# Row maxima of a gated attention kernel in two half-width matmuls: one single maximum a step, split between two places of the step

## The chip, the cores and the metric

The kernel runs on one core of a Trainium2 chip. The metric is the device time of one launch in microseconds (us). Engines are called TensorE (PE in the profile, its weight loads PEld), VectorE (DVE), ScalarE (ACT), GpSimd (POOL) and SyncE (SP); SyncE computes nothing here and issues DMAs.

## What is computed

The input x has 2048 rows of 512. Two attention branches with 32 heads of 16 read it, and a gate mixes their outputs:

```python
g = sigmoid((x * gate_w).sum(-1))
a = branch_A(x)      # 8 keys a query, at distances 0, 2, .. 14
# branch B: 32 heads of queries, one head of keys and values
q = (x @ wq) per head;  k = x @ wk;  v = x @ wv
p = softmax((q @ k.T) * 16 ** -0.5)       # 2048 keys for each query and head
b = (p @ v, heads side by side) @ wo
out = g * a + (1 - g) * b
```

Branch B's softmax needs the maximum of each row of 2048 scores before the exponential. The kernel computes the scores twice for that: once with queries on the partitions, only to take the maxima, and once with keys on the partitions, for the exponential.

## The kernel before, in words

**Units and steps.** Branch B is cut into 32 units (`NU`): 4 blocks of 512 queries times 8 groups of 4 heads. A unit has 16 steps (`NJ`), one for each 128 keys; 512 steps (`NS`) in all. Before a unit's first step its row maxima must be known: they are subtracted through two extra rows of the queries' operand `qst` (`shift_a`, `shift_c`, `shift_b`), so that the score matmuls of the second computation give shifted scores.

**A step** of the main loop (line 737 on) does: scores of the first two heads (`exp_pair`, L316, into a bank pair `pe`), their exponential on ScalarE (L318), scores and exponential of the other two heads, and the weighted sum of the step before (`weighted`, L326, four column tiles into `po`). The two heads of a pair lie on two row groups of the array (partitions 0 to 63 and 64 to 127), so that their matmuls run side by side.

**Maxima** are made in the gaps. A full set of maxima is 32 units x 32 slots; a slot is 512 keys for 128 queries of two heads. `fill_pair` (L269) makes a whole slot: two matmuls of 512 keys, one a row group, into the two banks of `m2` (called pm in the profile), and one VectorE reduce of 128x1024 (L274). `fill_one` (L278) makes half a slot, a "single": one matmul of 512 keys of one head into the one bank `m1` (called ps) and one reduce of 128x512 (L285). 64 such halves make a unit (`NF // NU`). In the step the order is written out: scores, pair, scores, single, weighted sum (`order`, L752; the first step after an output phase has the two scores swapped).

**Planner.** The order is fixed when the program is built, by hand-made clocks for TensorE, ScalarE and VectorE (`clk`, `after`) with the costs of line 42; `free` says when a bank is thought free. `fill_ready` makes a maximum if its bank is thought free within a slack (0.15) of TensorE's clock. `more` maxima as singles are made while the count still to make is above what the pairs alone would give (L766, L767). If a unit's maxima are late, `pause` makes them in the `pe` banks with nothing else going on. `tasks` are small pieces with a due time (shift, `finish_c`), run at the end of a step by `run_tasks`; `hooks` are those of branch A (`a_max`, `a_exp`, `a_sum`).

**When a unit's 64th half is made**, `filled` (L258) issues two small reduces (L264) and a 32x32 transposition (L266) on VectorE at once. ScalarE and VectorE then form the shift `ml` (L291, L297), and `shift_b` (L301) issues 8 small DMAs of it into `qst`: all on SyncE while branch A still has work on GpSimd, later 4 on SyncE and 4 on GpSimd.

**Around the steps.** A front stage (to about 316 us) makes the projections, with maxima of the first units between them; four output phases (`out_phase`) of 4 row blocks each multiply with wo, with pairs and singles between. Branch A runs on GpSimd beside all of this. SyncE also loads each unit's queries (`stack`, L231, two DMAs) and stores outputs (L501).

Of the kernel before, what the change touches and what calls it, by code (L numbers as in the profile page):

```python
# [13 lines left out]
P = 128  # L14
# [4 lines left out]
NJ = S // P  # L19
# [18 lines left out]
NS = NU * NJ  # L38
NF = 2 * NU * 2 * 4 * 4


T_R, T_LAT, T_EXP, T_RED2, T_RED1, T_W, T_LUMP, T_Q = 0.23, 0.20, 0.92, 1.14, 0.61, 1.18, 2.53, 3.2


@with_exitstack
def gated_mix_kernel(ctx, tc, xt, wa, wk, wq, wo_a, wo_b, out):
# [190 lines left out]
    slots += [(v, pr, t, kc) for v in range(2, NU) for pr in range(2) for t in range(4) for kc in range(4)]  # L237
    half = []
    free = {"m2": 0.0, "m1": 0.0, "e0": 0.0, "e1": 0.0, "po": 0.0}
    tasks, shifted = [], set()  # L240

    def fillable():
        return bool(half) or bool(slots) and slots[0][0] < len(stacked) and stacked[slots[0][0]] <= clk["pe"]
# [7 lines left out]
    def max_mm(dst, v, pr, t, kc, odd):  # L251
        b = 64 * odd
        nc.tensor.matmul(dst, qst[v % NB][b:b + 62, pr, t * P:(t + 1) * P], kst[b:b + 62, kc * 512:(kc + 1) * 512], start=True, stop=True)  # L253

    def to_go():
        return 2 * len(slots) + len(half)

    def filled(v, n):  # L258
        left[v] -= n
        if not left[v]:  # L260
            ms = wp.tile([P, 2, 2, 8], F32, name="ms")
            m = mx.pop(v).rearrange("p b i t k -> p b (i t) k")
            for x in range(2):
                nc.vector.tensor_reduce(ms[:, :, x, :], m, AX.X, ALU.max)  # L264
            mt = wp.tile([P, 32], F32, name="mt")
            nc.vector.transpose(mt, ms.rearrange("p b x y -> p (b x y)"))  # L266
            tasks.append((after("dve", 0, 0.5) + 0.1, shift_a, (v, mt)))

    def fill_pair(dst, key):  # L269
        v, pr, t, kc = slots.pop(0)  # L270
        m = unit_tile(v)
        for odd in range(2):
            max_mm(dst[:, odd, :], v, pr, t, kc, odd)
        nc.vector.tensor_reduce(m[:, :, pr, t, kc], dst, AX.X, ALU.max)  # L274
        free[key] = after("dve", after("pe", 0, T_R) + T_LAT, T_RED2) + 0.08
        filled(v, 2)

    def fill_one(dst=m1, key="m1"):  # L278
        if not half:
            v, pr, t, kc = slots.pop(0)  # L280
            half.extend([(v, pr, t, kc, 0), (v, pr, t, kc, 1)])
        v, pr, t, kc, odd = half.pop(0)
        m = unit_tile(v)
        max_mm(dst, v, pr, t, kc, odd)
        nc.vector.tensor_reduce(m[:, odd, pr, t, kc:kc + 1], dst, AX.X, ALU.max)  # L285
        free[key] = after("dve", after("pe", 0, T_R) + T_LAT, T_RED1) + 0.08
        filled(v, 1)

# [7 lines left out]
    def shift_c(v, mt, th, ml):  # L296
        nc.vector.scalar_tensor_tensor(ml, mt, mk[:, 5:6], th.bitcast(F32), op0=ALU.mult, op1=ALU.add)  # L297
        after("dve", 0, 0.2)
        shift_b(v, ml)

# [193 lines left out]
    def out_store(j, n, k):  # L494
# [4 lines left out]
        if n == C:  # L499
            nc.gpsimd.tensor_add(two[:, 0], two[:, 0], two[:, 1])  # L500
            nc.sync.dma_start(out[0].rearrange("(p j) d -> p j d", j=NJ)[:, j, :], two[:, 0])  # L501
# [57 lines left out]
    def fill_ready(key, slack):  # L559
        if fillable() and free[key] <= clk["pe"] + slack:  # L560
            clk["pe"] = max(clk["pe"], free[key])
            if key == "m1":
                fill_one()
            elif half and (not slots or half[0][0] < slots[0][0] or slots[0][0] >= len(stacked)):
                fill_one(m2[:, 0, :], "m2")
# [3 lines left out]
    def pause(most):  # L569
        n = 0  # L570
        while n < most and slots and fillable():
            key = min(("e0", "e1", "m2"), key=lambda k: free[k])
            clk["pe"] = max(clk["pe"], free[key])
            if half:
                fill_one({"e0": eb[0], "e1": eb[1], "m2": m2}[key][:, 0, :], key)
# [21 lines left out]

    def run_tasks():
        for task in [t for t in tasks if t[0] <= clk["pe"]]:
            tasks.remove(task)  # L600
            task[1](*task[2])

    def front_fills(slack, post=None, first=None):
# [36 lines left out]

    hooks, pool, done = [], 0.0, set()
    QK, AV = 12500, 22500
# [12 lines left out]
    def run_pool():  # L655
        nonlocal pool
        now = clk["pe"] * 1e3
        while pieces and pool < now + 3000:
# [13 lines left out]
            elif kind == "qk1":  # L672
                a_scores(g, 1)
                pool += QK
                hooks.append((pool + 6000, a_max, g, "max"))
            elif kind == "sub":
                a_sub(g)
                pool += 800
                hooks.append((pool + 4000, a_exp, g, "exp"))
                hooks.append((pool + 6500, a_sum, g, "sum"))  # L680
            elif kind == "wo":
# [3 lines left out]
            else:  # L685
                a_values(g)
                pool += AV
        for h in sorted(hooks, key=lambda h: h[0]):
            if h[0] <= now:
                hooks.remove(h)  # L690
                h[1](h[2])
                done.add((h[3], h[2]))

# [43 lines left out]
    for s in range(NS + 1):  # L737
# [9 lines left out]
        v = min(x[0][0] for x in (half, slots, [(NU,)]) if x)  # L747
        need = left.get(v, NF // NU)
        steps = 16 * v - 6 - s
        short = need - 2.8 * max(0, steps) if v < NU else 0  # L750
        lead = (NF - to_go()) / 64 - s / 16
        order = (0, "m2", 1, "m1") if s > 1 else (1, "m2", 0, "m1") if s else ()  # L752
        if not pieces and clk["pe"] * 1e3 > pool + 2000 and outs < NJ:
            n = C if outs < NJ - 4 else C - 1
            if s >= (16 * NHG * (outs // 4 + 1) + 4 if n == C else 16 * (NU - 2) + 4) and (lead < 1.6 or outs == 0 and s >= 400):
                out_phase(list(range(outs, outs + 4)), n)
                outs += 4
                order = (1, "m2", 0, "m1")
        elif short > 0 and steps < 2:
            pause(short)  # L760

        for which in order:
            if which == "m2":
                fill_ready("m2", 0.15)
            elif which == "m1":
                ahead = 2 * (16 * (NU - 2) - 8 - s) + 11 * (NJ - 4 - outs)  # L766
                if ahead < to_go() - NF // NU or s >= 16 * (NU - 2) - 8 and ahead + 64 < to_go():  # L767
                    fill_ready("m1", 0.15)
            elif s < NS:
                exp_pair(s, which)  # L770
# [6 lines left out]
    assert not slots and not half and not hooks and not tasks and outs == NJ, (len(slots), len(hooks), len(tasks), outs)  # L777

# [59 lines left out]
```

## Time and profile before

| | |
|---|---|
| median of 3 runs | 1558.52 us (1558.35 to 1559.88) |
| profiled execution | 1558.82 us |
| its span in the trace | 1557.0 us |
| front stage | to about 316 us |
| output phases | from about 1011, 1149, 1286 and 1460 us, 26 to 32 us each |
| last maximum reduced | 1492 us |

The span is the time from the first to the last instruction that the trace shows; the launch's own time is 1.8 us longer. In the profile's groups a row gives line, engine, operation, output and input, shapes and count, then busy time in us and mean ns of one, then the idle time ahead of them and what ended most of it. In the timeline a row gives start, length, engine, line, operation and, in brackets, the idle time before it and its releaser; rows of equal instructions side by side are merged (x2, x8). In the table of stretches a row gives the stretch, its length, busy time and count of the engines asked for, TensorE's granted clock, DMA share and GB/s.

### The profile page before, as it was taken

What the parts mean: (1) busy time and instruction counts of PE and PEld (TensorE: products, weight loads), DVE (VectorE), ACT (ScalarE), POOL (GpSimd) and SP (SyncE); (2) the same over time, 40 slices, a digit from 0 to 9 for tenths busy, and PEclk for the clock granted to TensorE, in tenths of its full rate; (3) what the DMA queues carried; (4) which work ended last, traced back from release to release, by engine and by line L of the source; (5) the groups of instructions that cost most, each with busy time, mean ns of one, the idle gap of its engine ahead of it and who ended that gap; (6) DMA issues with size and microseconds to landing.
All of it is one profiled execution on the core that took longest, in us unless ns stands there. A gap on an engine that the chain in (4) does not pass through costs nothing.

```text
span 1557.0 us, 25703 instructions
## 1 busy us (share of the span) xinstructions
PE 1525.7 (98%) x10076; PEld 703.8 (45%) x10076; DVE 1335.8 (86%) x1667; ACT 1120.9 (72%) x1315; POOL 834.2 (54%) x1015
## 2 busy tenths in 40 slices
PE   8999999999999999999999999999999999999998
PEld 4677777733333333333333333363354336333532
DVE  6899999979888898888899889898898889888731
ACT  4223111189999899999989998939966993999676
POOL 7420897778987898889887885240031004000210
PEclk9999999999999999999999999999999999999999
DMA  7842312211011101211111010000000000000000
GB/s 240 261 141 90 120 62 91 99 59 41 21 49 49 56 19 50 65 47 34 50 49 56 20 48 12 22 28 12 12 19 21 12 2 29 2 2 1 2 1 27
DMA packets 42889, 78.61 MB, mean 50 GB/s; under 512 B 8544, under 2 KB 25024, under 8 KB 40720
## 3 DMA queue, kind: packets, MB, share of 16 engines
q1 hardware_dynamic: 20224, 35.56, 7.9%
q0 software_dynamic: 4640, 26.99, 5.0%
q10 hardware_dynamic: 17904, 14.42, 2.8%
q8 instruction: 79, 1.29, 0.3%
q14 instruction: 42, 0.34, 0.1%
HBM read 46.96 MB, written 29.45 MB: 49 GB/s over the span
## 4 chain that ended last, share of the span: by engine, by line
PE 82%; DVE 12%; ACT 4%; issue 1%; DMA 0%; DVEq 0%; POOL 0%; ACTq 0%
PE po L326 30%; PE pe L316 21%; PE pm L253 9%; PE ps L253 8%; DVE mx L274 7%; PE pe L529 5%; DVE mx L285 4%; ACT pexp L318 3%; PE pl L159 3%; PE pl L160 2%; PE pl L161 2%; PE pl L167 1%; PE pl L253 1%; DVE ml L297 0%; PE po L253 0%
## 5 line engine op out<-in xcount | busy, mean ns | idle before, releaser
L318 ACT ACTIVATE pexp<-pe 128x1024 f32<-128x1024 f32 x1022 | 989.2, 1022 | 105.2 <-PE pe L316 100.4
L274 DVE TENSOR_REDUCE mx<-pm 128x2 f32<-128x1024 f32 x610 | 743.9, 1219 | 144.3 <-PE pm L253 140.9
L326 PE MATMUL po<-pexp,vst 128*32 128x512 f32 x4088 | 545.3, 605 | 0.7 <-ACT pexp L318 0.6
L316 PE MATMUL pe<-qst,kst 64*128 64x512 f32 x2044 | 467.0, 452 | 11.1 <-ACT pexp L318 5.8
L316 PEld LDWEIGHTS pe<-qst,kst 64*128 64x128 f32 x2044 | 191.1, 184 | 518.4 <-ACT pexp L318 506.2
L285 DVE TENSOR_REDUCE mx<-ps 128x1 f32<-128x512 f32 x597 | 405.5, 679 | 0.0
L253 PE MATMUL pm<-kst,qst 62*128 62x512 f32 x1230 | 262.6, 417 | 0.8 <-DVE mx L274 0.2
L253 PE MATMUL ps<-kst,qst 62*128 62x512 f32 x597 | 242.6, 406 | 0.4
L381 POOL TENSOR_TENSOR pr<-aext 128x512 f32<-128x512 f32 x128 | 163.9, 1302 | 57.1 <-DMA aext<-ad 57.0
L326 PEld LDWEIGHTS po<-pexp,vst 128*32 128x32 f32 x4088 | 80.4, 108 | 176.4 <-issue 163.3
L206 ACT ACTIVATE stage<-pl 128x384 f32<-128x384 f32 x64 | 31.5, 492 | 165.3 <-PE pl L161 162.8
L426 POOL TENSOR_TENSOR oa<-oa,av 128x512 f32<-128x512 f32 x112 | 143.5, 1281 | 8.8
L346 POOL TENSOR_TENSOR rl<-rl,gate_t 128x16 f32<-128x16 f32 x31 | 6.8, 220 | 242.6 <-DVE rl L342 242.6
L253 PEld LDWEIGHTS pm<-kst,qst 62*128 62x128 f32 x1230 | 117.4, 186 | 41.4 <-DVE mx L274 17.2
L253 PEld LDWEIGHTS ps<-kst,qst 62*128 62x128 f32 x597 | 111.1, 186 | 30.4 <-DVE mx L285 22.3
L424 POOL TENSOR_TENSOR av<-aext,lg 128x512 f32<-128x512 f32 x112 | 118.9, 1061 | 7.5
L305 POOL DMA_DIRECT2D qst<-ml x48 | 27.3, 573 | 134.6 <-DVE ml L297 130.8
L159 PE MATMUL pl<-wah,xh 128*128 128x384 f32 (+1 forms) x256 | 93.7, 366 | 0.4 <-ACT stage L206 0.4
L274 DVE TENSOR_REDUCE mx<-pl 128x2 f32<-128x1024 f32 x75 | 91.1, 1215 | 0.0
L160 PE MATMUL pl<-wal,xh 128*128 128x384 f32 (+1 forms) x256 | 87.1, 340 | 0.0
L161 PE MATMUL pl<-wah,xl 128*128 128x384 f32 (+1 forms) x256 | 86.9, 339 | 0.0
L529 PE MATMUL pe<-woh,turned 64*128 64x512 f32 x496 | 84.3, 400 | 0.1
(124 smaller groups left out, 1204.4 us busy)
## 6 DMA issues: line engine op xcount, KB each, us to landing
aext<-ad POOLq DMA_DIRECT2D x16, 1440.0 KB, 6.2
qst<-qd SPq DMA_DIRECT2D x64, 192.0 KB
ad<-stage ACTq DMA_DIRECT2D x32, 384.0 KB
qd<-qhi SPq DMA_DIRECT2D x32, 256.0 KB
xraw<-xt SPq DMA_DIRECT2D x16, 256.0 KB
qd<-qlo SPq DMA_DIRECT2D x16, 256.0 KB
qst<-ml SPq DMA_DIRECT2D x208, 2.0 KB
out<-two SPq DMA_DIRECT2D x12, 256.0 KB
```

The costliest lines, as they stand in the source:

```text
L159: mms.append(lambda c=c: nc.tensor.matmul(out_ap, ah(c), bh(c), start=(c == 0), stop=False))
L160: mms.append(lambda c=c: nc.tensor.matmul(out_ap, ah(c), bl(c), start=False, stop=False))
L253: nc.tensor.matmul(dst, qst[v % NB][b:b + 62, pr, t * P:(t + 1) * P], kst[b:b + 62, kc * 512:(kc + 1) * 512], start=True, stop=True)
L274: nc.vector.tensor_reduce(m[:, :, pr, t, kc], dst, AX.X, ALU.max)
L285: nc.vector.tensor_reduce(m[:, odd, pr, t, kc:kc + 1], dst, AX.X, ALU.max)
L316: nc.tensor.matmul(bank[:, odd, :], kst[b:b + 64, kt * P:(kt + 1) * P], qst[u % NB][b:b + 64, pr, :], start=True, stop=True)
L318: nc.scalar.activation(e, bank, AF.Exp, scale=SCALE)
L326: nc.tensor.matmul(po[32 * i:32 * i + 32, :], vst[:, kt, :], pexp[s, i // 2][:, i % 2, :], start=(kt == 0), stop=(kt == NJ - 1))
L381: nc.gpsimd.tensor_mul(pr[:, k], q, e[:, o:o + NJ, AC:2 * AC])
L424: nc.gpsimd.tensor_mul(av, e[:, o:o + NJ, 2 * AC:].rearrange("p j (h d) -> p j h d", d=DH), lg[:, w].unsqueeze(3).to_broadcast([P, NJ, AG, ...
L426: nc.gpsimd.tensor_add(ao, ao, av)
L529: nc.tensor.matmul(eb[x % 2][:, b, :], st[h], mv[h], start=first, stop=last)
```

## The change

1. A single maximum becomes 256 keys of both heads (`fill_two`, new) instead of 512 keys of one. The upper half of `m1` (odd head) is written by a matmul right behind the step's first scores; the lower half (even head) by another behind the second scores. One reduce of 128x512 follows as before. Between the two matmuls stands a no-op on SyncE that reads the upper half: it waits for the first matmul, and the second matmul waits for it. The planner puts the second at least 0.5 us after the first.
2. The pair (`fill_pair`) stays between the two scores, now behind the first half. Its slack is `M2S` 0.9 instead of 0.15. The first half is issued when `m1` is thought free within 0.3.
3. Maxima are kept for 256 keys, so the tile `mx` has 8 values a row where it had 4 (two buffers instead of three), and the unit's two closing reduces read twice as much. The pair's reduce writes four values. A slot half done is kept in `quarter`; `fill_apart` makes what is left of one in another bank.
4. VectorE's small pieces (closing reduces, shift, branch A's maximum and sum) become tasks of which a step runs at most one, and none if VectorE's clock is over 0.9 (`BEHIND`) past TensorE's. `shift_b`'s DMAs are issued at least 3 us (`SHD`) after the instruction that makes their data.
5. The 12 output stores of `out_store` go to GpSimd's queue instead of SyncE's. The planner's cost of the weighted sum goes from 1.18 to 1.21; `steps` counts to 8 steps ahead of a unit instead of 6.

The core of the diff:

```diff
+BEHIND = 0.9
+M2S = 0.9
+SHD = 3.0
-T_R, T_LAT, T_EXP, T_RED2, T_RED1, T_W, T_LUMP, T_Q = 0.23, 0.20, 0.92, 1.14, 0.61, 1.18, 2.53, 3.2
+T_R, T_LAT, T_EXP, T_RED2, T_RED1, T_W, T_LUMP, T_Q, T_Z = 0.23, 0.20, 0.92, 1.14, 0.61, 1.21, 2.53, 3.2, 0.14
...
-            mx[v] = wp.tile([P, 2, 2, 4, 4], F32, name="mx", bufs=3)
+            mx[v] = wp.tile([P, 2, 2, 4, 8], F32, name="mx", bufs=2)
...
         if not left[v]:
-            ms = wp.tile([P, 2, 2, 8], F32, name="ms")
...
+            tasks.append((clk["dve"], close, (v, mx.pop(v).rearrange("p b i t k -> p b (i t) k"))))
+
+    def close(v, m):
+        ms = wp.tile([P, 2, 2, 8], F32, name="ms")
+        for x in range(2):
+            nc.vector.tensor_reduce(ms[:, :, x, :], m, AX.X, ALU.max)
+        mt = wp.tile([P, 32], F32, name="mt")
+        nc.vector.transpose(mt, ms.rearrange("p b x y -> p (b x y)"))
+        tasks.append((after("dve", clk["pe"], 0.66) + 0.1, shift_a, (v, mt)))
...
+    def fill_two():
+
+        if not quarter:
+            v, pr, t, kc = slots.pop(0)
+            quarter.extend([(v, pr, t, kc, 0), (v, pr, t, kc, 1)])
+        v, pr, t, kc, h = quarter.pop(0)
+        m = unit_tile(v)
+        max_mm(m1[:, 256:512], v, pr, t, kc, 1, 256 * h, 256)
+        nc.sync.keepalive_nop([nc.sync.lower_ap(m1[:, 256:512])])
+        at = clk["pe"] + 0.5
+
+        def low():
+            clk["pe"] = max(clk["pe"], at)
+            max_mm(m1[:, 0:256], v, pr, t, kc, 0, 256 * h, 256)
+            nc.vector.tensor_reduce(m[:, :, pr, t, 2 * kc + h], m1.rearrange("p (o n) -> p o n", o=2), AX.X, ALU.max)
+            free["m1"] = after("dve", after("pe", 0, T_Z) + T_LAT, T_RED1) + 0.08
+            filled(v, 1)
+
+        return low
...
         nc.vector.scalar_tensor_tensor(ml, mt, mk[:, 5:6], th.bitcast(F32), op0=ALU.mult, op1=ALU.add)
-        after("dve", 0, 0.2)
-        shift_b(v, ml)
+        tasks.append((after("dve", clk["pe"], 0.45) + SHD, shift_b, (v, ml)))
...
-        at = after("dve", clk["pe"] + T_LAT, 0.8)
+        at = after("dve", clk["pe"] + T_LAT, 0.96)
...
-            nc.sync.dma_start(out[0].rearrange("(p j) d -> p j d", j=NJ)[:, j, :], two[:, 0])
+            nc.gpsimd.dma_start(out[0].rearrange("(p j) d -> p j d", j=NJ)[:, j, :], two[:, 0])
...
+    def run_tasks(spread=False):
+
         for task in [t for t in tasks if t[0] <= clk["pe"]]:
+            small = task[1] in (close, shift_c, finish_c, a_max, a_sum)
+            if small and spread == 2 or spread and small and clk["dve"] > clk["pe"] + BEHIND:
+                continue
             tasks.remove(task)
             task[1](*task[2])
+            if small:
+                spread = spread and 2
...
-        for which in order:
-            if which == "m2":
-                fill_ready("m2", 0.15)
-            elif which == "m1":
...
+        if order and s < NS:
+            exp_pair(s, order[0])
+            low = None
+            if more and (quarter or slots) and not half and fillable() and free["m1"] <= clk["pe"] + 0.3:
+                low = fill_two()
+            fill_ready("m2", M2S)
+            exp_pair(s, order[1])
+            low and low()
+        else:
+            fill_ready("m2", M2S)
+        if more and half:
+            fill_ready("m1", 0.3)
...
-        run_tasks()
+        run_tasks(True)
```

`close`, `finish_c`, `a_max` and `a_sum` take 0.66, 0.6, 0.4 and 0.6 us of VectorE's planner clock, `finish_a` 0.96.

More of the change, by code (lines that the diff above doesn't have):

```diff
@@ L570, in pause @@
         n = 0
-        while n < most and slots and fillable():
+        while n < most and fillable():
             key = min(("e0", "e1", "m2"), key=lambda k: free[k])
             clk["pe"] = max(clk["pe"], free[key])
+            if quarter:
+                fill_apart({"e0": eb[0], "e1": eb[1], "m2": m2}[key], key)
+                n += 1
+                continue
             if half:
@@ L687, in run_pool @@
                 pool += AV
[L688 to L692, printed above, removed]
     lumps += [("q", m) for m in range(2, 4 * NQB)]
@@ L746, in gated_mix_kernel @@
                     assert pause(4)
-        v = min(x[0][0] for x in (half, slots, [(NU,)]) if x)
+        v = min(x[0][0] for x in (half, quarter, slots, [(NU,)]) if x)
         need = left.get(v, NF // NU)
-        steps = 16 * v - 6 - s
+        steps = 16 * v - 8 - s
         short = need - 2.8 * max(0, steps) if v < NU else 0
         lead = (NF - to_go()) / 64 - s / 16
-        order = (0, "m2", 1, "m1") if s > 1 else (1, "m2", 0, "m1") if s else ()
+        order = (0, 1) if s > 1 else (1, 0) if s else ()
         if not pieces and clk["pe"] * 1e3 > pool + 2000 and outs < NJ:
@@ L757, in gated_mix_kernel @@
                 outs += 4
-                order = (1, "m2", 0, "m1")
+                order = (1, 0)
         elif short > 0 and steps < 2:
             pause(short)
-        for which in order:
-            if which == "m2":
-                fill_ready("m2", 0.15)
-            elif which == "m1":
[L766 to L770, printed above, removed]
+        ahead = 2 * (16 * (NU - 2) - 8 - s) + 11 * (NJ - 4 - outs)
+        more = ahead < to_go() - NF // NU or s >= 16 * (NU - 2) - 8 and ahead + 64 < to_go()
+        if order and s < NS:
[10 more added lines that the diff above has]
+            fill_ready("m1", 0.3)
         if s:
@@ L774, in gated_mix_kernel @@
                 finish_a(u - 1, nc.gpsimd)
-        run_tasks()
+        run_tasks(True)
         run_pool()
-    assert not slots and not half and not hooks and not tasks and outs == NJ, (len(slots), len(hooks), len(tasks), outs)
+    assert not slots and not half and not quarter and not tasks and outs == NJ, (len(slots), len(tasks), outs)
     for x in range(8):
```

44 lines of the change are left out of this document (25 added, 19 removed).

## The prediction

> **What bounds the kernel now.** I read the page first: engine shares, chain and groups.
>
> ```profile
> span 1557.0 us, 25703 instructions
> PE 1525.7 (98%) x10076; PEld 703.8 (45%) x10076; DVE 1335.8 (86%) x1667; ACT 1120.9 (72%) x1315; POOL 834.2 (54%) x1015
> ...
> PE 82%; DVE 12%; ACT 4%; issue 1%; DMA 0%; DVEq 0%; POOL 0%; ACTq 0%
> ...
> L318 ACT ACTIVATE pexp<-pe 128x1024 f32<-128x1024 f32 x1022 | 989.2, 1022 | 105.2 <-PE pe L316 100.4
> L274 DVE TENSOR_REDUCE mx<-pm 128x2 f32<-128x1024 f32 x610 | 743.9, 1219 | 144.3 <-PE pm L253 140.9
> ...
> L285 DVE TENSOR_REDUCE mx<-ps 128x1 f32<-128x512 f32 x597 | 405.5, 679 | 0.0
> ```
>
> TensorE is the bound on average, VectorE next. An average hides the stages, so the second view is one ordinary step of the main loop in the timeline (start, length, engine, line).
>
> ```profile
> 1379.62 0.50 PE L316 MATMUL pe<-qst,kst 64*128 64x512 f32 x2
> 1379.95 0.40 PE L253 MATMUL pm<-kst,qst 62*128 62x512 f32 x2
> 1380.19 0.41 PE L316 MATMUL pe<-qst,kst 64*128 64x512 f32 x2
> 1380.22 1.94 ACT L318 ACTIVATE pexp<-pe 128x1024 f32<-128x1024 f32 x2 [0.20 <-PE pe L316]
> 1380.39 1.23 DVE L274 TENSOR_REDUCE mx<-pm 128x2 f32<-128x1024 f32 x1 [0.31 <-PE pm L253]
> 1380.43 0.39 PE L253 MATMUL ps<-kst,qst 62*128 62x512 f32 x1
> 1380.75 1.06 PE L326 MATMUL po<-pexp,vst 128*32 128x512 f32 x8
> 1381.54 0.68 DVE L285 TENSOR_REDUCE mx<-ps 128x1 f32<-128x512 f32 x1
> 1381.75 0.50 PE L316 MATMUL pe<-qst,kst 64*128 64x512 f32 x2
> ```
>
> A step lasts 1381.75 - 1379.62 = 2.13 us and TensorE is never free in it: 0.33 to the pair of maxima (pm), 0.24 to the second scores, 0.24 to the single (ps), 0.32 to the weighted sum (po), 1.00 to the next scores. ScalarE needs 1.94 of it. VectorE idles 0.31, and the reason matters below: its pair reduce follows the pm matmul by 1380.39 - 1379.95 = 0.44, the single's reduce follows 1380.39 by 1.15 and ends at 1382.22, after the next step's pm (which needs only the pair reduce) has been issued. The third view counts the stages: single reduces (L285) in the front stage and in the four stretches of steps between the output phases, then the front's pair reduces (L274), then the weighted sums (L326) of the first stretch.
>
> ```profile
> 0.00:316.00 316.00, 93.76 (x146) 0.99 0.43 137
> 316.00:1009.20 693.20, 216.71 (x319) 1.00 0.13 41
> 1045.50:1148.00 102.50, 32.61 (x48) 1.00 0.06 16
> 1184.00:1284.50 100.50, 31.93 (x47) 1.00 0.03 8
> 1321.00:1458.20 137.20, 35.32 (x52) 1.00 0.01 3
> ```
> ```profile
> 0.00:316.00 316.00, 181.83 (x155) 0.99 0.43 137
> ```
> ```profile
> 316.00:1009.20 693.20, 339.99 (x2552) 50.19 (x2552) 1.00 0.13 41
> ```
>
> The four stretches take 1033.4 us and hold 466 singles. The first has 2552 / 8 = 319 steps and one single in each: 693.20 / 319 = 2.173 us a step, 0.04 above the clean one. The granted clock is 1.00 in all four. So a unit of 16 steps costs 34.8 us, and 466 / 16 = 29.1 units' worth of steps carry singles.
>
> **The change, part by part.** *The single becomes two halves.* What it removes: a half streams 256 columns on one row group while the other group streams something else; half of the 0.24 spacing is 0.12, so at most 0.12 a step, 466 x 0.12 = 56 us. That is the gain in sight. ScalarE allows it nearly all: in the last steps, which have no maxima, two steps run from one row to the other below in 4.02 us, 2.01 each.
>
> ```profile
> 1522.36 0.99 PE L316 MATMUL pe<-qst,kst 64*128 64x512 f32 x4
> ...
> 1526.38 0.99 PE L316 MATMUL pe<-qst,kst 64*128 64x512 f32 x4
> ```
>
> What it moves: the first half, U, is issued ahead of pm, where the single stood behind the second scores. U writes the bank ps, so it waits until the previous step's single reduce has read it; and everything behind U on TensorE, pm first, waits with it. An output phase shows such a wait.
>
> ```profile
> 1024.80 0.68 DVE L285 TENSOR_REDUCE mx<-ps 128x1 f32<-128x512 f32 x1
> ...
> 1025.53 0.18 PEld L253 LDWEIGHTS ps<-kst,qst 62*128 62x128 f32 x1 [0.25 <-DVE mx L285]
> 1025.54 0.29 PEld L529 LDWEIGHTS pe<-wol,turned 64*128 64x128 f32 x2
> 1025.56 0.47 PE L253 MATMUL ps<-kst,qst 62*128 62x512 f32 x1
> ```
>
> The reduce ends at 1025.48; the weight load starts 0.05 later; the matmul ends at 1026.03, and 0.39 before that is 1025.64, so it really streams 0.11 after its load. The load behind it (L529) came only after it. Now the loop for two steps running that both have a U: U to the end of its columns 0.12 (pm's second head shares its row group), pm to its reduce 0.44, pair reduce to single reduce 1.15, single reduce 0.68, hand-over 0.05, load 0.11, next U: **2.55 us**, against 2.13. VectorE stands idle from the end of one single reduce to the start of the next pair reduce, 0.72 us, since pm now sits behind U. Today pm is issued while the single reduce runs. This is the wait that takes the place of the one removed.
>
> The Trainium skill, "TensorE: Matmul & The Clock Gate", Part 3 (The mechanism), gives TensorE a 64-deep window that pulls weight loads ahead of matmuls in flight. If that let pm's loads and matmuls pass a waiting U, the loop would open and the step would be 2.06. The rows of 1025.53 and 1025.54 show a load behind a waiting load not passing it, so I don't count on it.
>
> *How many steps have a U.* The planner issues one if it thinks ps free within 0.3 of its TensorE clock. By its constants, with the step at 0: scores to 0.23, pair to 0.46, reduce 0.66 to 1.80, second half at 0.73 to 0.87, reduce to 2.41, ps free at 2.49, weighted to 2.08; the limit is 2.08 + 0.23 + 0.3 = 2.61. So it issues a U in each step and takes the delay for nothing. A small VectorE piece over 0.45 uses up that 0.12 (0.33 of it lies in the idle time) and makes one step skip: the unit's close (0.66), the transposition after a unit (0.96), finish_c (0.6, every second unit), a_sum (0.6, 16 in all), about 3 in 16 steps.
>
> SyncE's shortest instruction in the timeline, an output store's issue:
>
> ```profile
> 1296.93 0.36 SPq L501 DMA_DIRECT2D out<-two  x1
> ```
>
> A U with no U in the next step costs: 0.33, then U to the no-op 0.44 - 0.12 = 0.32, no-op 0.05, hand-over 0.05, load 0.11, second half 0.12, drain 0.32 - 0.24 = 0.08, weighted sum 1.00: 2.06. The no-op itself isn't in the trace: from nothing up to that 0.36; I take a hand-over's 0.05, since it moves nothing. At 0.36 these three steps a unit cost 0.9 us more, 27 us in all; in the 2.55 loop the second half has 0.49 of slack and hides it. A step without U costs 2.01. A unit: 10 x 2.55 + 3 x 2.06 + 3 x 2.01 = 37.7 us, +2.94; x 29.1 = **+86 us**.
>
> *The maxima not made.* 3 x 29.1 = 87 singles are lost to skipped steps. The last stretch has 52 singles in 137.2 / 2.13 = 64 steps and can take 12. The other 75 have to be made in pauses, where TensorE and ScalarE do nothing else and VectorE's pair reduce sets the pace: 75 x 1.15 / 2 = **+43 us**.
>
> *SyncE's queue.* The no-op stands in order behind the shift's DMAs.
>
> ```profile
> 365.37 5.22 SPq L305 DMA_DIRECT2D qst<-ml  x8
> ```
> ```profile
> 1210.74 2.60 SPq L305 DMA_DIRECT2D qst<-ml  x4
> ```
> ```profile
> L305 POOL DMA_DIRECT2D qst<-ml x48 | 27.3, 573 | 134.6 <-DVE ml L297 130.8
> ...
> qst<-ml SPq DMA_DIRECT2D x208, 2.0 KB
> ```
>
> 32 units make 256 issues, 48 of them on POOL, so 12 units have 4 on SyncE and 20 have 8. The front stage closes 7 of the 20 ((146 + 2 x 155) / 64). In the other 13 the next no-op comes 5.22 + 0.05 after the last instead of 2.55: 2.72 late, less the slack of the second half (next U at 2.55; 0.53 + 0.12 + 0.08 + 1.00 + 0.33 = 2.06): 2.2 x 13 = **+29 us**. What queues behind it on TensorE is the weighted sum and the next scores, and ScalarE waits for those. Four issues, 2.60, fall within the slack. SyncE waiting for ml, which holds no one today, would hold the no-op; the 3 us delay of shift_b covers that.
>
> *The rest, at nothing.* The pair reduce writes 4 values for 2 from the same 1024 elements. The close reads 128 for 64 elements a call: by 679 ns for 512 and 1219 for 1024 that is 67 ns x 64 calls = 4 us, in VectorE's idle 0.72; uncovered, 4 us. Spreading the small pieces could win back the 0.04 of each step (19 us), but in the loop above they lie in idle time already. The 12 output stores move to POOL's queue at 573 ns each, 7 us if POOL, 54% busy, were ever the last. Twice as many weight loads for singles: pairs follow each other at 0.24 with loads of 0.19 recorded, so loads are hidden; I take nothing.
>
> The skill's same page, section LDWEIGHTS (loading the stationary operand), makes a load depend on its columns alone, 128 / 1.2 = 107 ns. One more load a single, if it could not hide behind a 256-column half, would be 466 x 0.107 = 50 us by that page, on top of the sum; the 0.24 spacing speaks against it.
>
> **Sum:** 86 + 43 + 29 = 158 on the profiled execution's 1558.82 (span 1557.0 and 1.8 around it): **1717 us**. The median, 1558.52, lies 0.3 below that execution, which changes nothing.
>
> **The rivals.** *Faster: U is never late.* If the single reduce ended in time, every step would cost 2.06: 466 x (2.173 - 2.06) = -53. The point that decides is whether ps is free 0.17 after a step's first scores (0.33 less 0.16 for hand-over and load); by the rows it comes 0.33 + 2.39 = 2.72 after the previous ones, 0.49 past 2.06 + 0.17. For it: the planner's own clock says 2.08. Against: each term of the 2.55 is a row. SyncE's issues then cost 13 x 3.2 + 12 x 0.6 = 49 at most, so 1506 to 1555; I put it at 1530. With the whole 49 it is *the same*: 1555.
> *The planner skips every other step.* Then no two U are neighbours: 233 x 2.06 + 245 x 2.01 = 972 for 1033, -61, but 233 - 12 = 221 maxima go to pauses, +127, and some +13 on SyncE: 1638. For it: the margin is only 0.12. Against: most steps have no small piece.
> *U in every step*, no skips: 466 x (2.55 - 2.173) = +176, and 29: 1764.
>
> **How the numbers follow.** Forecast (1670 to 1750) 0.54; every other step (1600 to 1670) 0.14; every step (1750 to 1790) 0.12; faster 0.15; within 0.2%, about what a measurement of this kernel can tell from no change, 0.05. Range 1600 to 1790 holds 0.80, with the no-op's upper bound and a smaller overlap of U and pm (2.43 for 2.55, -35 us) inside it. Faster 0.15, same 0.05, slower 0.80.
>
> **What would show it.** Right: weight loads of ps waiting for the single reduce some 0.4 us in most steps, over 100 us in all (now 22); VectorE idle about 0.7 ahead of each pair reduce, its share near 78%; steps of 2.5 in runs with some of 2.0 between; maxima into the banks pe, which there are none of now; 13 steps with a stall of 2 us behind eight SyncE issues. Wrong: steps of 2.1 with TensorE still full, or pm starting ahead of a waiting U.

## The result and the profile after

The changed kernel takes **1728.57 us** (median of 4 runs, 1725.72 to 1733.24) against 1559.2 for the kernel before in the same comparison (4 runs, 1558.35 to 1561.45). The ratio is 1.1087, with a 95% interval of 1.1063 to 1.1111: slower by about 11%. The profiled execution took 1733.24 us, with a span of 1731.5.

The page of the changed kernel, in the order of the page shown of before:

```profile
span 1731.5 us, 27405 instructions
...
PE 1587.7 (92%) x10510; PEld 782.6 (45%) x10510; DVE 1342.6 (78%) x1651; ACT 1150.4 (66%) x1315; POOL 839.7 (48%) x1027
...
PE 46%; DVE 23%; issue 21%; SPq 4%; ACT 3%; DMA 1%; POOL 1%; DVEq 0%; ACTq 0%; POOLq 0%
...
L352 ACT ACTIVATE pexp<-pe 128x1024 f32<-128x1024 f32 x1022 | 1018.0, 1023 | 242.3 <-PE pe L350 234.8
L279 DVE TENSOR_REDUCE mx<-pm 128x4 f32<-128x1024 f32 x621 | 756.5, 1218 | 291.0 <-PE pm L256 284.9
...
L308 DVE TENSOR_REDUCE mx<-ps 128x2 f32<-128x512 f32 x421 | 287.0, 682 | 18.5 <-PE ps L256 18.5
```

VectorE does the same work as before (1342.6 us for 1335.8) in a span that is 174.5 us longer, and its idle time ahead of the pair reduce has doubled, from 140.9 to 284.9 us. The chain that ended last was 82% TensorE; now TensorE has 46%, and VectorE, "issue" and SyncE's queue hold half of it. That is the mark of a loop: one engine waits for another, which waits for the first.

Two steps in the timeline show the loop. In them, L256 into ps are the halves, L256 into pm the pair, L350 the scores.

```profile
562.62 0.28 PE L256 MATMUL ps<-kst,qst 62*128 62x256 f32 x1
...
563.72 0.68 DVE L308 TENSOR_REDUCE mx<-ps 128x2 f32<-128x512 f32 x1
...
563.83 0.49 PE L350 MATMUL pe<-qst,kst 64*128 64x512 f32 x2
...
564.46 0.18 PEld L256 LDWEIGHTS ps<-kst,qst 62*128 62x128 f32 x1 [0.45 <-DVE mx L308]
...
564.46 0.29 PEld L256 LDWEIGHTS pm<-kst,qst 62*128 62x128 f32 x2
...
565.11 1.22 DVE L279 TENSOR_REDUCE mx<-pm 128x4 f32<-128x1024 f32 x1 [0.70 <-PE pm L256]
...
566.98 0.18 PEld L256 LDWEIGHTS ps<-kst,qst 62*128 62x128 f32 x1 [0.56 <-DVE mx L308]
```

The halves' reduce ends at 564.40, and only then does the next first half load its weights (564.46). The pair's banks had been read by 563.81 (the pair reduce of 562.58 with its 1.23), yet the pair's loads stand behind the half's and start with it. VectorE, done at 564.40, gets the pair at 565.11. From one first half to the next: 566.98 - 564.46 = 2.52.

The waits of the whole run, in total, times and longest:

```profile
DVE mx L279 <- PE pm L256: 284.9, 381, 6.9
...
PEld ps L256 <- DVE mx L308: 170.2, 323, 0.6
...
PE ps L256 <- DVE mx L308: 68.7, 279, 0.3
...
PEld ps L256 <- SPq L302: 31.5, 20, 2.9
```

Where the 174.5 us of span went, by cutting both traces at the first scores of each step: the ordinary steps sum to 1205.8 us now and 1076.8 before, +129. The output phases and pauses, each with the slow step behind it, sum to 191.1 and 147.3, +44. The front stage is 1.5 longer. The two sums do not hold the same steps: 494 are ordinary now and 501 before, since seven more lie in or behind the pauses. Seven steps at the mean of before, 2.15 us, are 15 us; counted step for step, the steps cost +144 and the phases and pauses +29.

### The profile page after: what moved, and what is told of

The parts are those of the page before. It is cut to its first block, busy times and chain, and to the rows that moved or that the text cites. A ratio compares the mean times of both kernels' runs of the same rounds, so it can differ in the third digit from the quotient of the medians.

```text
span 1731.5 us, 27405 instructions
## 1 busy us (share of the span) xinstructions
PE 1587.7 (92%) x10510; PEld 782.6 (45%) x10510; DVE 1342.6 (78%) x1651; ACT 1150.4 (66%) x1315; POOL 839.7 (48%) x1027
## 4 chain that ended last, share of the span: by engine, by line
PE 46%; DVE 23%; issue 21%; SPq 4%; ACT 3%; DMA 1%; POOL 1%; DVEq 0%; ACTq 0%; POOLq 0%
DVE mx L308 11%; PE po L360 11%; PE ps L256 9%; PE pm L256 8%; PE pe L350 8%; DVE mx L279 7%; SPq L339 4%; PE pe L563 3%; DVE mx L290 3%; ACT pexp L352 3%; PE pl L162 2%; PE pl L163 2%; PE pl L164 2%; PE pl L170 1%; DMA qd<-qhi 1%
## 5 line engine op out<-in xcount | busy, mean ns | idle before, releaser
L352 ACT ACTIVATE pexp<-pe 128x1024 f32<-128x1024 f32 x1022 | 1018.0, 1023 | 242.3 <-PE pe L350 234.8
L279 DVE TENSOR_REDUCE mx<-pm 128x4 f32<-128x1024 f32 x621 | 756.5, 1218 | 291.0 <-PE pm L256 284.9
L350 PE MATMUL pe<-qst,kst 64*128 64x512 f32 x2044 | 512.2, 458 | 23.8 <-DMA qst<-ml 9.7
L350 PEld LDWEIGHTS pe<-qst,kst 64*128 64x128 f32 x2044 | 237.1, 188 | 477.5 <-ACT pexp L352 375.5
L256 PE MATMUL ps<-kst,qst 62*128 62x256 f32 (+1 forms) x986 | 337.1, 342 | 94.8 <-DVE mx L308 68.7
L256 PE MATMUL pm<-kst,qst 62*128 62x512 f32 (+1 forms) x1264 | 345.5, 441 | 3.3 <-DVE mx L279 2.6
L308 DVE TENSOR_REDUCE mx<-ps 128x2 f32<-128x512 f32 x421 | 287.0, 682 | 18.5 <-PE ps L256 18.5
L256 PEld LDWEIGHTS ps<-kst,qst 62*128 62x128 f32 x986 | 184.7, 187 | 240.2 <-DVE mx L308 170.2
L256 PEld LDWEIGHTS pm<-kst,qst 62*128 62x128 f32 x1264 | 171.2, 188 | 43.6 <-issue 17.1
L290 DVE TENSOR_REDUCE mx<-ps 128x2 f32<-128x512 f32 x144 | 97.7, 679 | 1.6 <-PE ps L256 1.6
L279 DVE TENSOR_REDUCE mx<-pl 128x4 f32<-128x1024 f32 x74 | 89.7, 1212 | 0.0
```

Source lines behind the costliest of these rows:

```text
L279: nc.vector.tensor_reduce(m[:, :, pr, t, 2 * kc:2 * kc + 2], dst.rearrange("p o (h n) -> p o h n", h=2), AX.X, ALU.max)
L290: nc.vector.tensor_reduce(m[:, odd, pr, t, 2 * kc:2 * kc + 2], dst.rearrange("p (h n) -> p h n", h=2), AX.X, ALU.max)
L308: nc.vector.tensor_reduce(m[:, :, pr, t, 2 * kc + h], m1.rearrange("p (o n) -> p o n", o=2), AX.X, ALU.max)
L350: nc.tensor.matmul(bank[:, odd, :], kst[b:b + 64, kt * P:(kt + 1) * P], qst[u % NB][b:b + 64, pr, :], start=True, stop=True)
L352: nc.scalar.activation(e, bank, AF.Exp, scale=SCALE)
```

## The experiments

Each diff is against the changed kernel, unless it says otherwise. The kernel before ran beside each: its medians were 1558.02 us (9 runs; with the first four experiments), 1559.08 (1 run; with the second four) and 1557.65 (15 runs; with the last four). "A step with halves" is one of the steps of the main loop that hold a pair and both halves; in the changed kernel there are 410, with a median of 2.527 us.

**e1: the reduce of the halves reads other data.**

```diff
+            nc.sync.keepalive_nop([nc.sync.lower_ap(m1[:, 0:256])])
-            nc.vector.tensor_reduce(m[...], m1.rearrange("p (o n) -> p o n", o=2), AX.X, ALU.max)
+            nc.vector.tensor_reduce(m[...], kst[:, 0:512].bitcast(F32).rearrange("p (o n) -> p o n", o=2), AX.X, ALU.max)
```

> The changed kernel, but the reduce of the two halves reads a constant SBUF tile of the same shape instead of the bank ps (so these maxima are left out of the result and the softmax shift is another), and a second SyncE no-op behind the second half keeps the bank's two writers apart. The first half U then waits for no reduce. Theory (U waits for the last single reduce and holds pm behind it, 2.55 us a step): the waits of ps on VectorE are gone, steps are 2.06 to 2.1 us, 421 x 0.45 = -190 us, SyncE's eight and four issues cost some 15 us more than now because the steps are shorter: about 1554. Rival (the no-op's way over SyncE, or twice the matmuls and weight loads, make the step long): steps stay at 2.4 or above, 1690 or more.

Measured: 1620.44 us. The step in the timeline:

```profile
560.01 0.50 PE L351 MATMUL pe<-qst,kst 64*128 64x512 f32 x2
...
560.36 0.28 PE L256 MATMUL ps<-kst,qst 62*128 62x256 f32 x1
...
560.90 1.23 DVE L279 TENSOR_REDUCE mx<-pm 128x4 f32<-128x1024 f32 x1 [0.29 <-PE pm L256]
...
562.05 0.50 PE L351 MATMUL pe<-qst,kst 64*128 64x512 f32 x2
```

TensorE's instructions are the same; what is gone is the first half's wait for the reduce, and with it the reduce's wait for the second half. That gives a step of 2.04 here and a median of 2.096, and the pair reduce's idle time is 0.29 instead of 0.70. So the loop through the reduce is what makes 2.53. The time itself missed the forecast of 1554 by 66 us: the mean step is 2.264, well over its median. The waits say what is left:

```profile
PEld ps L256 <- SPq L302: 44.2, 20, 4.0
```

That is the no-op behind the shift's DMAs, and its stalls lengthen steps to as much as 7 us. They are longer than in the changed kernel (31.5 us, at most 2.9); that a shorter step hides less of a stall is argued. The other remainder is the pauses (54.2 us for the first output phase with its pause, steps of 14.1 and 10.5), hardly shorter than in the changed kernel.

**e2: the first half behind the pair.** Then a late bank holds up no pair.

```diff
             exp_pair(s, order[0])
+            fill_ready("m2", M2S)
             low = None
...
                 low = fill_two()
-            fill_ready("m2", M2S)
```

> The changed kernel with one thing moved: the first half is issued behind the pair pm instead of ahead of it. Theory: pm no longer stands behind the wait, the loop is open; what is left is TensorE's own order, 0.33 to pm, 0.24 to the first half, 0.53 to the second half over SyncE, 0.20 to the weighted sum, 1.00: 2.30 us a step, 421 x 0.23 = -97, about 1630. Rival (doubled matmuls and weight loads cost the time): 1729, unchanged. Second rival (the way over SyncE is nearer 0.3 than 0.53): 2.1 a step, about 1555.

Measured: 1685.05 us; 447 steps with halves, median 2.253 (forecast 2.30), mean 2.439. The step came out; the total did not, for the same SyncE stalls. A step from its middle:

```profile
702.78 0.29 PE L256 MATMUL ps<-kst,qst 62*128 62x256 f32 x1
...
703.16 0.18 PEld L256 LDWEIGHTS ps<-kst,qst 62*128 62x128 f32 x1 [0.18 <-SPq L302]
...
703.47 0.16 PEld L360 LDWEIGHTS po<-pexp,vst 128*32 128x32 f32 x8
```

SPq L302 is the no-op. The timeline leaves it out, but asked for its line the trace has it (length in ns: least, median, most):

```profile
L302 SPq EVENT_SEMAPHORE  x451: 17/17/28, 314.7 to 1529.6; - x151
```

From the start of the first half to the second half's load 0.38 us pass. 0.29 of it is the first half's own recorded length and 0.017 the no-op, so the price is that of letting the first half end before the second starts, not the no-op's. Here the weighted sum stands behind it: it starts 0.69 us after the second scores (these too start at 702.78), where the step of before has 0.56 (1380.19 to 1380.75). In the changed kernel's loop the same wait is covered.

**e3: the halves alone**, put into the kernel before: no-op, eight maxima, `fill_apart`; no spreading, no delay of the shift's DMAs, the output stores on SyncE.

```diff
-        tasks.append((after("dve", clk["pe"], 0.45) + SHD, shift_b, (v, ml)))
+        after("dve", 0, 0.2)
+        shift_b(v, ml)
...
-            nc.gpsimd.dma_start(out[0].rearrange("(p j) d -> p j d", j=NJ)[:, j, :], two[:, 0])
+            nc.sync.dma_start(out[0].rearrange("(p j) d -> p j d", j=NJ)[:, j, :], two[:, 0])
...
-            fill_ready("m2", M2S)
+            fill_ready("m2", 0.15)
...
-        run_tasks(True)
+        run_tasks()
```

> The kernel before with only the halves and what they need (the no-op, 8 maxima a row, fill_apart); small pieces unspread, slack 0.15, output stores and shift DMAs as before. Theory: the halves carry the whole loss: 1700 to 1760. Rival (the spread pieces, the slack of 0.9 or the moved stores cost it): 1540 to 1600.

Measured: 1811.78 us (4 runs), ratio 1.1625, interval 1.161 to 1.1641: over the range expected. The ordinary step is the same, 2.528 in the median, so the halves set it and nothing else of the change. What is added lies on SyncE's own queue:

```profile
SPq L335 <- DVE ml L327: 270.9, 31, 34.0
SPq L531 <- POOL two L530: 103.6, 12, 16.2
```

SyncE waits for the shift's data (L335; 201.4 us in 10 waits in the changed kernel) and for the output rows (L531; none there), and the no-op stands behind it. The weight loads' waits for the no-op rise from 31.5 to 89.9 us, the longest from 2.9 to 6.0. The changed kernel is 83 us faster than this; 58 of them lie in the ordinary steps (mean 2.682 for 2.541, 414 and 410 of them), where the medians are equal and the long ones, of 7 to 9.6 us, are such stalls. So the delay of the DMAs and the moved stores clear the queue that the halves need. The prediction had named that use of the delay; for the stores it had only GpSimd's time, at nothing. This run also takes out the slack of 0.9 and the spreading, so the shares, and those of the other 25 us, aren't told apart.

**e4: the single put back**, behind the second scores, with everything else of the change.

```diff
-            low = None
-            if more and (quarter or slots) and not half and fillable() and free["m1"] <= clk["pe"] + 0.3:
-                low = fill_two()
             fill_ready("m2", M2S)
             exp_pair(s, order[1])
-            low and low()
+            if more:
+                fill_ready("m1", 0.15)
```

> The changed kernel with the single back as it was, 512 keys of one head behind the second scores; all the rest of the change stays (spread small pieces, slack 0.9, late shift DMAs, stores on POOL). Theory: steps of 2.13 us, and of the 0.03 to 0.04 a step that clumped small pieces cost before, some is won: 1540 to 1560. Rival (the planner's other changes cost time): over 1600.

Measured: 1566.2 us (5 runs), ratio 1.0056, interval 1.0042 to 1.007; median step 2.133, as before the change. It misses the expected bound by 6 us, through one stall:

```profile
503.00 0.42 ACT L440 ACTIVATE lg<-lg 128x256 f32<-128x256 f32 x1 [4.17 <-POOL lg L436]
```
```profile
504.38 0.79 PE L350 MATMUL pe<-qst,kst 64*128 64x512 f32 x2 [3.78 <-ACT pexp L352]
...
506.44 1.93 PE L360 MATMUL po<-pexp,vst 128*32 128x512 f32 x8
```

ScalarE took branch A's exponential before GpSimd had its data, TensorE idled 3.78 us, and the weighted sum behind it took 1.93 instead of 1.07. The two steps from 498.41 us on took 5.97 and 3.93, together 5.6 more than two median steps.

**e5: e1 with all of the shift's DMAs on GpSimd's queue.**

```diff
-                (nc.gpsimd if b and not pieces else nc.sync).dma_start(...)
+                nc.gpsimd.dma_start(...)
```

> As the run with the reduce on a constant SBUF tile (the halves' maxima are left out of the result), and all the shift DMAs go to POOL's queue, so that the no-ops on SyncE have nothing long ahead of them. Theory (steps of 2.10 us without the wait of ps; what that run lost beyond it, 2.264 less 2.096 in 410 steps = 69 us, is the no-op behind SyncE's issues): about 1550, no step over 3 us outside output phases and pauses. Rival (those long steps come from something else): 1610 or more.

Measured: 1650.2 us, slower than e1 by 30.

```profile
ACT lg L441 <- POOL lg L437: 77.4, 14, 11.6
...
PEld ps L256 <- SPq L302: 0.4, 2, 0.2
```

The weight loads' wait for the no-op falls from 44.2 us to 0.4: those stalls are SyncE's issues, as the theory says. The total does not show it. The first step starts at 336.7 us instead of 312.8, which is 24 of the 30, and ScalarE waits for GpSimd for 77.4 us (13.0 in e1).

**e6: the changed kernel with all of the shift's DMAs on GpSimd's queue** (the diff of e5, without e1's).

> The changed kernel with all shift DMAs on POOL's queue and nothing else changed. Theory: the wait of ps on the single reduce stays (steps of 2.53), only the stalls behind SyncE's issues go, 34 us in the long steps and the half clock that follows them: 1670 to 1695. Rival (SyncE's queue is the main cost of the change): 1600 or below.

Measured: 1725.46 us. The total says "no gain"; the stages (length, TensorE, weight loads, VectorE, ScalarE, GpSimd, clock) say something else.

```profile
0.00:341.40 341.40, 308.82 (x1463) 226.32 (x1463) 290.64 (x366) 81.75 (x186) 220.10 (x271) 0.97 0.40 127
341.40:1708.20 1366.80, 1262.20 (x9008) 551.19 (x9008) 1044.11 (x1269) 1065.65 (x1125) 736.01 (x964) 0.99 0.08 25
```
```profile
0.00:319.80 319.80, 304.11 (x1464) 222.74 (x1464) 290.45 (x366) 81.84 (x186) 191.83 (x222) 0.99 0.42 136
319.80:1716.60 1396.80, 1275.16 (x9010) 555.70 (x9010) 1045.84 (x1269) 1065.18 (x1125) 647.85 (x806) 0.98 0.08 25
```

The second pair of rows is the changed kernel's. The main stage gains 30.0 us, about the forecast's 29 for SyncE's queue; the wait for the no-op is 0.4 us in all here too. The front stage, in which GpSimd now has 28.3 us more to do, loses 21.6. That leaves 8 against the changed kernel's profiled 1733.24.

**e7: the first half only with a margin**, so that every other step has halves.

```diff
-            ... and free["m1"] <= clk["pe"] + 0.3:
+            ... and free["m1"] + 0.3 <= clk["pe"]:
```

> The changed kernel, but the planner issues the first half only if it thinks ps free 0.3 us before, not up to 0.3 us after. Some 240 halves fewer are then made in steps and as many in pauses. Theory: hardly two steps running have a first half, so the wait of ps on the reduce is nearly gone and steps are 2.0 to 2.1; pauses cost 240 x 1.15 / 2 = 139 us: 1640 to 1690. Rival (halves are dear in themselves, by the no-op or by doubled matmuls): the steps with halves stay at 2.5, and with the pauses the time is 1750 or more.

Measured: 1718.27 us, outside the expected range. The 453 steps outside pauses, 226 with halves (median 2.236) and 227 without (1.900), took 971.6 us, 2.14 each. The prediction's rival had 972 for 478 steps, 2.03 each, so that the two totals agree is chance. The eleven pauses, with the steps over 3 us right behind them and without the ordinary steps that these stretches contain, take some 163 us where the changed kernel's three take 24. There are 249 halves' reduces for 421, so 172 maxima more, made mainly in pauses, cost some 139 us, 0.8 each where the forecast had 0.575. The waits show two reasons:

```profile
PE pe L350 <- DMA qst<-ml: 43.7, 6, 7.8
PEld pe L256 <- DVE mx L279: 42.8, 46, 1.4
```

A pause ends with up to 7.8 us in which TensorE waits for the shift's DMA, and in it TensorE, waiting for reduces, falls to half clock (0.67 granted in the pause from 844.3 to 868.3).

**e8: VectorE's small pieces not spread.**

```diff
-        run_tasks(True)
+        run_tasks()
```

> The changed kernel with the small pieces of VectorE run when due, several in a step if they fall so. Theory: they lie in the 0.7 us a step that VectorE idles in the loop, so spreading them or not makes no difference: 1715 to 1745. Rival (spreading is what keeps the halves on time): 1760 or more.

Measured: 1729.2 us, median step 2.527: no difference. The spreading wins nothing in the loop, where the small pieces lie in VectorE's idle time.

**e9: the shift's DMAs two a step**, over four steps of the main loop, on the same queues as in the change.

```diff
+        for k in range(4):
+            tasks.append((clk["pe"] + 2.05 * k, shift_d, (v, ml, two[2 * k:2 * k + 2], k == 3)))
+
+    def shift_d(v, ml, items, last=True):
+        for eng, b, g in items:
+            dst = qst[v % NB][64 * b + 62:64 * b + 64].rearrange("x i (t q) -> x i t q", t=4).bitcast(F32)
+            eng.dma_start(dst[:, :, :, 32 * g:32 * g + 32], ml[...].bitcast(F32))
```

> The changed kernel with the shift's DMAs in the main loop issued two a step over four steps, on the engines that had them, instead of eight (later four) at once; the front stage is as it was. A no-op then has at most 1.3 us of issues ahead of it, less than a step. Theory: the loop over the single reduce stays (steps of 2.53), the stalls behind SyncE go: -30 us in the long steps and some 10 to 20 of half clock after them, 1680 to 1700. Rival (the long steps have another cause): 1725 or more.

Measured: 1693.7 us, 34.9 below the changed kernel's median. Nothing is left out and no queue is relieved of work; the halves only never meet more than two issues.

```profile
PEld ps L256 <- SPq L302: 6.9, 20, 1.2
```

The median step stays at 2.525 and the mean falls from 2.541 to 2.462; the granted clock rises from 0.979 to 0.992. So SyncE's queue costs about 35 us, with the half clock that follows its stalls; 6.9 us of its waits are left.

**e10: e1 and e9 together.**

> Both costs removed: the reduce of the two halves reads a constant SBUF tile (these maxima are left out of the result), and the shift's DMAs are issued two a step. Theory: steps of 2.10 without long ones, so 1620 - 69 = about 1550, with the pauses still in it. Rival (the long steps of the run with the constant tile come from something else): 1610 or more.

Measured: 1583.92 us: between the expectation and the rival. The step is 2.102 in the median, 2.169 in the mean. Steps of 3.3 us remain, about one a unit. In them the issues have run together: the row below merges eight, of which the first four follow each other without a break (570.38 to 572.99) and the others in twos. The halves wait up to 2.2 us:

```profile
570.38 6.57 SPq L350 DMA_DIRECT2D qst<-ml  x8
```
```profile
PEld ps L256 <- SPq L302: 24.8, 21, 2.2
```

The pauses and the slow steps behind them take about 36 us, six ordinary steps included. With the loop cut and the issues spread, then, the change is still not faster than 1557.65.

**e11: e2 and e9 together**: the version with the halves and all of their work that came closest.

> The first half behind the pair, and the shift's DMAs two a step. Theory: steps of 2.25 us without long ones: 1685 less 447 x 0.186 = 83, about 1600, still slower than the kernel before, since the way over SyncE between the halves costs more than the 0.12 us that they save. Rival (with both waits gone the halves win): 1555 or below.

Measured: 1626.77 us; 447 steps with halves, median 2.253, mean 2.316. Theory and rival were both wrong, by some 27 us or more. The step stays longer than the step of before (2.253 against 2.133): ordering the halves costs more than the 0.12 us that they were to save. The place is that of e2, 0.69 us from the second scores (700.70) to the weighted sum (701.39).

**e12: e4 with branch A's exponential due 3 us later.**

```diff
-                tasks.append(((pool + 4000) / 1e3, a_exp, (g,), ("exp", g)))
-                tasks.append(((pool + 6500) / 1e3, a_sum, (g,), ("sum", g)))
+                tasks.append(((pool + 7000) / 1e3, a_exp, (g,), ("exp", g)))
+                tasks.append(((pool + 9500) / 1e3, a_sum, (g,), ("sum", g)))
```

> The changed kernel with the single back as it was and branch A's exponential and sum due 3 us later. The run with the single back lost 5.7 us where ScalarE waited for POOL's subtraction and TensorE then ran at half clock. Theory (that one wait is most of the 8 us): 1557 to 1562, no difference from before that can be told. Rival (the spread pieces or the slack cost it): 1564 or more.

Measured: 1556.96 us (11 runs) against 1557.65 (15 runs), ratio 0.9994, interval 0.9982 to 1.0005. The rest of the change, without the halves, is worth nothing that can be measured, and e4's 8 us were mostly that one wait (5.6 us in its two steps). No version here beats the kernel before measurably.

## Why the prediction was right, step by step

**The loop.** The order of the 2.55 is that of the rows above (reduce, half's load, pair, pair reduce 0.70 later where the forecast had 0.72, reduce), and the measured step is 2.527 in the median. e1, which takes out the wait and leaves TensorE's work as it is, gives 2.096; the forecast had 2.06 for such a step. If the forecast's other terms are right, the 0.04 between them is all that is left for twice as many weight loads: 0.04 x 410 = 16 us, where the prediction named 50 for loads that nothing hid. No run takes the second load out alone. The no-op, which the forecast put at 0.05, takes 0.017. The pair's loads did not pass the waiting half's (564.46), so the reordering of loads that the Trainium skill describes ("TensorE: Matmul & The Clock Gate", Part 3) did not open the loop.

**The steps without a first half.** The forecast had 3 in 16; there are 62 beside 410, 2.1 in 16. And a step with halves behind such a step was to take 2.06: it takes 2.24 in the median, since the pair's banks are late there.

```profile
603.67 1.21 DVE L279 TENSOR_REDUCE mx<-pm 128x4 f32<-128x1024 f32 x1
...
604.94 0.19 PEld L256 LDWEIGHTS pm<-kst,qst 62*128 62x128 f32 x2 [0.36 <-DVE mx L279]
```

A small piece that makes a step skip also delays its pair reduce; the forecast let it delay the single alone. Both errors push up; that a step without halves takes 1.90 in the median and not 2.01 pushes down, but less. The steps' +144 less the stalls' 34 (next) is +110, where the forecast had +86.

**SyncE's queue.** Forecast 13 stalls of 2.2 us, 29 in all. The trace has 14 units with such a stall between 330 and 1061 us, 18 steps over 3 us, and what these take above 2.53 sums to 34; e9 gives 35. The place is as forecast:

```profile
605.05 5.24 SPq L339 DMA_DIRECT2D qst<-ml  x8
```
```profile
607.70 0.49 PE L350 MATMUL pe<-qst,kst 64*128 64x512 f32 x2
610.40 0.38 PE L256 MATMUL ps<-kst,qst 62*128 62x256 f32 x1 [2.21 <-SPq L302]
610.71 1.73 PE L360 MATMUL po<-pexp,vst 128*32 128x512 f32 x8
612.38 0.80 PE L350 MATMUL pe<-qst,kst 64*128 64x512 f32 x2
```

The eight issues end at 610.29 and the second half loads at 610.40. What the forecast lacked is the last two rows: behind the gap TensorE works at half clock, the weighted sum takes 1.73 instead of 1.07 and the scores 0.80 instead of 0.50. That is why a second step is over 3 us in four of the units.

**The pauses.** Forecast +43; measured +29 for phases and pauses, counted step for step. The forecast was too high, and it had one mechanism where there are two. The first pause (1085 to 1093 us) is paced by VectorE as forecast, TensorE waiting from pair to pair:

```profile
1089.10 0.79 PE L256 MATMUL pe<-kst,qst 62*128 62x512 f32 x2 [0.63 <-DVE mx L279]
1090.22 0.80 PE L256 MATMUL pe<-kst,qst 62*128 62x512 f32 x2 [0.34 <-DVE mx L279]
```

The second, of 14.5 us with its two steps, makes two pairs and then waits for the shift:

```profile
1613.42 2.58 SPq L339 DMA_DIRECT2D qst<-ml  x4
...
1617.18 1.00 PE L350 MATMUL pe<-qst,kst 64*128 64x512 f32 x2 [7.43 <-DMA qst<-ml]
```

From the pause's last pair, through the pair reduces, the closing reduces, the transposition, the shift and its DMAs, to the scores, TensorE has nothing to do for 7.43 us. The forecast costed a pause by its maxima alone. The other two pauses have no such end: the scores behind them wait 1.5 and 1.6 us for the pauses' last reduces. Fewer maxima were missing than the 75 of the forecast: the three pauses make eleven pairs (six in the banks pe, five in pm) and two half slots, 24 when counted as singles. By the forecast's price these are 14 us. So two errors worked against each other, too many maxima and too low a price for each; e7, where 172 more were missing, has the price at 0.8.

**The sum.** The steps were forecast 24 us too low, the stalls 5 too low and the pauses 14 too high. The loop, which was most of the forecast, came out as predicted, in its order and in its 2.55 us; that the total came within 12 us of the measured median is in part luck.

**The rest, at nothing.** For the spreading that holds (e8). For the DMA delay and the moved stores it holds only without the halves (e12). Given the halves, the changed kernel is 83 us faster than e3, and the weight loads' waits for the no-op, 58 us longer there, say that most of it is theirs; only the delay's part was in the prediction.

**The rivals.** *U is never late* falls with the rows of 564.46; with the loop cut it was still not faster (e10: 1583.92), and its bound of 1555 left the pauses out. *Every other step* did not happen, and e7 made it happen: 1718.27, not 1638. *U in every step* is refuted by the 62. No run cuts the pauses alone, so their price is read from the traces.

## What to carry to other kernels

When an instruction is moved ahead of others on an in-order engine, ask when what it waits for is released, and put that time beside the next step's start: a wait that cost nothing at the end of a step costs the whole step at its front, because everything behind it waits too. A plan's own clock that allows a slack of 0.3 us takes that delay for nothing, and only the loop through all engines shows it. A synchronization through a queue that also issues DMAs costs what stands in that queue, so price the queue's longest run of issues, not the no-op.

## What the runs showed of the hardware

TensorE's granted clock halves after short gaps, which the prediction left out. Behind 2.21 us without a matmul the weighted sum took 1.73 us (1.07 at full clock), behind 3.78 us it took 1.93 (e4), and in the pause of 1085 to 1093 us, behind gaps of 0.47 to 0.63 us, three running, a pair took 0.80 instead of 0.50. The stretch behind the first of these was granted 0.82 on average, an ordinary stretch 1.00:

```profile
606.70:616.00 9.30, 6.94 (x41) 2.89 (x39) 4.34 (x6) 4.24 (x6) 8.75 (x8) 0.82 0.01 2
1137.60:1229.60 92.00, 85.32 (x604) 35.01 (x604) 69.89 (x87) 76.70 (x78) 6.27 (x12) 1.00 0.05 13
```

The Trainium skill, "TensorE: Matmul & The Clock Gate", Part 1 (The HAM clock gate), lets the clock fall after at least one idle window of about 3.4 us. The 2.21 us gap is shorter than that, so here a window that is idle in part was enough; the measurement decides. The length of one gap does not decide alone. Of the changed kernel's fourteen stalls, the six of 2.2 us and more were all followed by half clock, the four of about 1.0 us or less never, and of the four between 1.38 and 1.53 us two were:

```profile
388.81 0.38 PE L256 MATMUL ps<-kst,qst 62*128 62x256 f32 x1 [1.38 <-SPq L302]
389.12 1.93 PE L360 MATMUL po<-pexp,vst 128*32 128x512 f32 x8
```
```profile
779.17 0.38 PE L256 MATMUL ps<-kst,qst 62*128 62x256 f32 x1 [1.45 <-SPq L302]
779.48 1.07 PE L360 MATMUL po<-pexp,vst 128*32 128x512 f32 x8
```

Two matmuls of 256 columns, ordered by a no-op on SyncE, are 0.38 us apart from the start of the first to the second's weight load (e2): 0.29 is the first one's recorded length, 0.017 the no-op. Eight DMAs of 2 KB hold SyncE for 5.24 us. Where the same DMAs go through GpSimd's queue, the front stage grew by 21.6 us (e6), with 28.3 us more of GpSimd's time in it; that the one makes the other is argued, not shown.
